# Splitting the last transfer of values in a streaming attention decode kernel

## The chip, the cores and the metric

The kernel runs on one core of one Trainium2 chip. The metric is the device time of one execution in microseconds (us), given as the median of several executions. A profile is one further execution, taken by the hardware profiler; its span (first to last instruction) is 1.7 to 1.9 us shorter than the device time. All times of landings and of single instructions below are from the records of such a trace, counted from the start of its span. A transfer has landed when the shares of all sixteen DMA engines have arrived: in the trace of the kernel before each of the last five values transfers has sixteen landings, 3.59 to 3.71 us from first to last. The record names different chips for different calls of runs (4, 2, 14 and 10), so times are compared with the kernel before in the same rounds; the traces, one per kernel, are from several chips.

## The reference, cut to what matters

Two attention decode steps with one query position and batch 4, their outputs concatenated. Part A has 32 query heads over 8 shared key/value heads and looks at the last 2048 positions; part B has 32 heads of its own and looks at all 8192. B is nearly all of the work: its two caches are 537 MB in bf16, every byte is used once, and the work on it is a matrix-vector product per head.

```python
q = (x @ wq).reshape(B, 1, 32, 128).transpose(0, 2, 1, 3)
scores = einsum("bhqd,bhkd->bhqk", q, k_cache) * 128 ** -0.5
o = einsum("bhqk,bhkd->bhqd", softmax(scores), v_cache)
out = o.transpose(0, 2, 1, 3).reshape(B, 1, 32 * 128) @ wo
```

## The kernel before

Part B goes in 64 chunks of two heads of one batch entry. A chunk is 128 tiles of keys and 128 tiles of values; a tile is 128 partitions x 128 values in bf16, so a chunk of keys or of values is 4 MB, one row of 32 KB for each partition. The sync queue (SP) issues all large loads. PE transposes the key tiles, multiplies them with the query, and multiplies the value tiles of the chunk before with its probabilities.

The last chunk of values has no later work to hide behind. It comes in five transfers with a semaphore each, so that PE can follow the stream:

```python
LASTV = (64, 32, 16, 8, 8)
...
def dma_kv(kind, c):
    ...
    if kind == "v" and c == NC - 1:
        j0 = 0
        for i, n in enumerate(LASTV):
            x = slice(j0 * P, (j0 + n) * P)
            sch.add_dma("sp", lambda e, x=x: e.dma_start(dst[:, x], src[:, x]), "d_vl%d" % i, waits=waits, key=("vl", j0))
            j0 += n
        return
...
def emit_pv(c, g):                       # eight products of a value tile with probabilities
    ...
    for t in range(TG):
        j = g * TG + t
        ...
        if c == NC - 1:
            waits += [("vl", j)] if ("vl", j) in sch.tk else []
        pe_mm(po[:, base:base + n], tile_of("v", c, j), pbt[...][:, c % NPB, j * UC:j * UC + n],
              start=j == 0, stop=j == ch["NT"] - 1, waits=waits, ...)
```

After its issues, the sync queue does one more thing. It waits for the output weights and for the last piece of keys (`kl`), and then raises a semaphore without which PE may not do the output product of an earlier chunk pair, in the middle of the last chunk's keys:

```python
dma_kv(kind, c)
if kind == "v" and c > NCA and (c - NCA) % 2 == 1:
    hp = max(0, c - NCA - 2) // 4
    sch.add("sp", lambda e: e.sem_inc(sems["eng_sp"], 1), waits=[("wos", hp)] + (["kl"] if c == NC - 1 else []),
            key=("wos2", c - 2 if c > NCA + 1 else NONE), self_inc=True)
```

## Time and profile before

| | before |
|---|---|
| time, median of 3 | 1374.14 us (1374.09 to 1374.22) |
| span of the profiled execution (its time was 1374.43 us) | 1372.6 us |
| HBM read, rate over the span | 587.21 MB, 428 GB/s |
| last values transfer landed, in the trace | 1369.060 us |
| last product of a value tile started | 1369.326 us |

The lines themselves are in the prediction. They are read from the outside in: the front page says which resource is busy all the time (the DMA engines), the chain of work says what the end hangs on (the last transfer), and the timeline says what is still to do when that has landed (eight products and a fixed rest). In a line of the chain or timeline the first number is the start and the second the duration, xN is a count, and brackets hold the idle time just before and what ended it. PE is the matrix unit, PEld its weight load, DVE, ACT and POOL are the vector, scalar and GpSimd engines; SPq is the sync queue, and a DMA_DIRECT2D there is the issue of a transfer. The end of a matmul is modelled, so each one shows 0.19 us although they start some 0.03 us apart. This hides short idle times.

### The profile page before, as it was taken

How to read it: one execution, taken by the hardware profiler on the slowest of the kernel's cores; microseconds unless marked ns; L12 is line 12 of the kernel's file. 1: busy time of each engine (PE TensorE's matmuls, PEld its weight loads, DVE VectorE, ACT ScalarE, POOL GpSimd, SP SyncE). 2: the span in 40 equal slices, each digit the busy share in tenths (PEclk: the TensorE clock that was granted, in tenths of full speed). 3: DMA queues.
4: the chain of work that ended last, by engine and by line, in shares of the span. 5: the costliest groups of instructions: out<-in, count | busy, mean ns of one | idle time of the engine just before them, and what ended most of it. 6: DMA issues, size and time to landing. Idle time of an engine off the chain costs nothing.

```text
span 1372.6 us, 59967 instructions
## 1 busy us (share of the span) xinstructions
PE 1176.5 (86%) x27065; PEld 1132.9 (83%) x27067; DVE 656.6 (48%) x1434; ACT 434.7 (32%) x650; POOL 7.3 (1%) x28
## 2 busy tenths in 40 slices
PE   4888898889888888988888888888898888888888
PEld 4777898888888888888888878888898888888888
DVE  1775454445444444454445444444454444444544
ACT  1553232333223322332233323322333233323322
POOL 2000000000000000000000000000000000000000
PEclk9998999999999999999999999999999999999999
DMA  9999999999999999999999999999999999999998
GB/s 400 423 424 432 429 433 428 433 432 432 432 431 433 429 434 428 434 430 434 430 434 430 430 433 432 432 431 433 429 433 431 434 429 434 430 432 432 432 427 352
DMA packets 25261, 587.53 MB, mean 428 GB/s; under 512 B 2820, under 2 KB 2840, under 8 KB 6296
## 3 DMA queue, kind: packets, MB, share of 16 engines
q1 hardware_dynamic: 25208, 587.22, 99.8%
q8 instruction: 16, 0.26, 0.1%
q14 instruction: 5, 0.04, 0.0%
q10 hardware_dynamic: 32, 0.01, 0.0%
HBM read 587.21 MB, written 0.01 MB: 428 GB/s over the span
## 4 chain that ended last, share of the span: by engine, by line
DMA 65%; PE 33%; issue 1%; DVE 1%; ACT 0%; SPq 0%; DVEq 0%
DMA kv<-in_B_k_cache_dram 57%; PE tr L408 21%; PE sc L410 9%; DMA kv<-in_A_k_cache_dram 5%; DMA kv<-in_B_v_cache_dram 3%; PE po L410 2%; PE fin L410 1%; PE ms L410 0%; ACT kt L476 0%; DVE sA L527 0%; SPq L365 0%; ACT pba L597 0%; PE ms L408 0%; DVE zA L683 0%; DVE rm L536 0%
## 5 line engine op out<-in xcount | busy, mean ns | idle before, releaser
L408 PE MATMUL tr<-identb,kv 128*128 128x128 bf16 x8704 | 697.9, 230 | 148.8 <-DMA kv<-in_B_k_cache_dram 141.5
L478 DVE COPY kt<-tr 128x1024 bf16<-128x1024 bf16 x736 | 502.6, 690 | 457.1 <-PE tr L408 452.7
L408 PEld LDWEIGHTS tr<-identb,kv 128*128 128x128 bf16 x8704 | 552.9, 104 | 165.2 <-DMA kv<-in_B_k_cache_dram 81.7
L476 ACT ACTIVATE kt<-tr 128x1024 bf16<-128x1024 bf16 x352 | 359.3, 1023 | 666.8 <-PE tr L408 666.7
L410 PE MATMUL sc<-qb,kt 128*128 128x64 bf16 x8704 | 446.2, 196 | 14.3 <-ACT kt L476 12.8
L410 PEld LDWEIGHTS sc<-qb,kt 128*128 128x128 bf16 x8704 | 366.4, 100 | 26.0 <-ACT kt L476 20.2
L410 PE MATMUL po<-pbb,kv 128*128 128x64 bf16 x8320 | 284.4, 192 | 4.5 <-issue 3.9
L410 PEld LDWEIGHTS po<-pbb,kv 128*128 128x128 bf16 x8320 | 263.2, 97 | 7.1 <-issue 4.1
L577 ACT ACTIVATE pbb<-sc,negb 64x128 bf16<-64x128 f32 x128 | 51.6, 403 | 254.3 <-DVE negb L564 253.5
L541 DVE TENSOR_REDUCE rm<-sc 64x1 f32<-64x128 f32 x128 | 37.0, 289 | 56.6 <-PE sc L410 55.7
L553 DVE TENSOR_REDUCE gm<-ms 1x2 f32<-1x128 f32 (+1 forms) x72 | 20.1, 279 | 48.4 <-PE ms L408 48.4
L564 DVE COPY negb<-ms 128x1 f32<-128x1 f32 (+1 forms) x72 | 11.4, 158 | 47.0 <-PE ms L410 46.8
L410 PE MATMUL ms<-identf,gx 1*128 1x1 f32 (+1 forms) x144 | 27.2, 256 | 0.8 <-DVE zA L683 0.8
L666 DVE TENSOR_TENSOR oz<-po,rz 128x8 bf16<-128x8 f32 x33 | 5.5, 166 | 40.7 <-PE po L410 40.7
L410 PEld LDWEIGHTS ms<-identf,gx 1*128 1x128 f32 (+1 forms) x144 | 21.1, 182 | 4.6 <-DVE zA L683 0.9
L577 ACT ACTIVATION_READ_ACCUMULATOR pbb<-sc,negb 64x1 f32 x128 | 23.7, 185 | 0.0
L410 PE MATMUL po<-pba,kv 128*128 128x64 bf16 x512 | 20.5, 199 | 3.5 <-issue 2.1
L410 PEld LDWEIGHTS po<-pba,kv 128*128 128x128 bf16 x512 | 17.9, 102 | 5.7 <-ACT pba L597 4.2
L408 PE MATMUL ms<-identf,rm 128*1 128x128 f32 (+1 forms) x72 | 19.5, 271 | 2.4 <-DVE rm L536 2.3
L557 DVE TENSOR_SCALAR gx<-gm 1x128 f32<-1x128 f32 (+1 forms) x72 | 16.0, 222 | 2.5
L683 DVE CAST zB<-ms 64x8 bf16<-64x8 f32 x64 | 10.5, 164 | 9.2 <-PE ms L410 8.7
L410 PE MATMUL ms<-xT,kv 128*128 128x4 bf16 x256 | 7.1, 166 | 8.8 <-DMA kv<-in_A_wq_dram 5.0
(61 smaller groups left out, 173.9 us busy)
## 6 DMA issues: line engine op xcount, KB each, us to landing
kv<-in_B_k_cache_dram SPq DMA_DIRECT2D x63, 4096.0 KB, 26.5
kv<-in_B_v_cache_dram SPq DMA_DIRECT2D x63, 4096.0 KB, 30.9
kv<-in_A_k_cache_dram SPq DMA_DIRECT2D x8, 2048.0 KB, 14.8
kv<-in_A_v_cache_dram SPq DMA_DIRECT2D x8, 2048.0 KB, 16.2
kv<-in_A_wq_dram SPq DMA_DIRECT2D x1, 4096.0 KB, 12.5
kv<-in_B_wq_dram SPq DMA_DIRECT2D x1, 4096.0 KB, 27.1
wor<-in_A_wo_dram SPq DMA_DIRECT2D x8, 512.0 KB, 9.8
wos<-in_B_wo_dram SPq DMA_DIRECT2D x16, 256.0 KB, 20.3
```

Of the source, the lines that this page charges most:

```text
L408: sch.add("pe", lambda e: e.transpose(o, l, r), waits, key)
L410: sch.add("pe", lambda e: e.matmul(o, l, r, start=start, stop=stop), waits, key)
L476: sch.add("act", lambda e: e.activation(dst, src, ACTF.Copy), waits=waits, key=("ev", s))
L478: sch.add("dve", lambda e: e.tensor_copy(dst, src), waits=waits, key=("ev", s))
L541: sch.add("dve", lambda e, src=src, pp=pp: e.tensor_reduce(out=rm[pp, m, 0:1], in_=src, axis=AX.X, op=ALU.max), waits=[("S", ch["s_last"]) ...
L553: sch.add("dve", lambda e: e.tensor_reduce(out=gm[0:C, m, 0:U], in_=src, axis=AX.X, op=ALU.max), waits=[("trm", c)], key=("gmax", c))
L557: sch.add("dve", lambda e: e.tensor_scalar(out=dst, in0=gv, scalar1=-scale, scalar2=None, op0=ALU.mult), waits=[("gmax", c)], key=("gx", c))
L564: sch.add("dve", lambda e: e.tensor_copy(negb[:, m, 0:C], ms[:, col:col + C]), waits=[("bc", c)], key=("negb", c))
L577: sch.add("act", lambda e, src=src, pp=pp, n=n, u=u: e.activation(probs_of(c)[pp, :, u], src, ACTF.Exp, bias=negb[pp, m, 0:1], scale=scale ...
L666: sch.add("dve", lambda e: e.tensor_tensor(out=o, in0=i0, in1=i1, op=ALU.mult), waits=waits, key=("oT", c))
L683: sch.add("dve", lambda e, src=src, pp=pp: e.tensor_copy(z[pp, :].rearrange("p (r b) -> p r b", r=k), src), waits=[("sm", c)] + free if h ...
```

## The change

The intent: the work behind the last landing is eight products. If the last eight tiles come in two transfers of four, the first four can be multiplied while the last four are on their way. The whole change is one line; the transfers, their semaphores and PE's waits all follow from it.

```diff
-LASTV = (64, 32, 16, 8, 8)
+LASTV = (64, 32, 16, 8, 4, 4)
```

## The prediction

> **What bounds the kernel now.** I read the front page first, then the list of transfers, then the chain of work that ended last, and at the end the timeline and the stretches of the last ten microseconds. The front page says what fills the span:
>
> ```profile
> span 1372.6 us, 59967 instructions
> PE 1176.5 (86%) x27065; PEld 1132.9 (83%) x27067; DVE 656.6 (48%) x1434; ACT 434.7 (32%) x650; POOL 7.3 (1%) x28
> DMA  9999999999999999999999999999999999999998
> HBM read 587.21 MB, written 0.01 MB: 428 GB/s over the span
> ```
>
> The DMA engines are busy 90% or more of every slice but the last, and move 428 GB/s from start to end; PE is below them at 86%. So the kernel is a stream of 587 MB, and the time is that stream plus a lead-in plus what is left to do after the last byte. The change touches no bytes and no stage but the last. The chain of work, asked for the last 73 us, shows that tail:
>
> ```profile
> 1329.92 39.14 DMA kv<-in_B_v_cache_dram
> 1369.06 0.05 issue
> 1369.11 0.42 PE po L410 x8
> ...
> 1369.62 0.18 DVE oz L666
> 1369.80 0.04 issue
> 1369.84 0.40 PE fin L410 x4
> 1370.24 0.02 issue
> 1370.27 0.42 DVE outB L724
> ```
>
> The reader is to see that the end hangs on the landing of the fifth and last values transfer (1329.92 + 39.14 = 1369.06), and that what follows is a fixed chain of 3.5 us: eight value products, the normalisation, four output products, one copy, the store. Only the first of these, 0.42 us, is what the change can shorten. The timeline of the same stretch, PE alone:
>
> ```profile
> 1366.85 2.03 PE L410 MATMUL po<-pbb,kv 128*128 128x64 bf16 x56
> 1369.11 0.41 PE L410 MATMUL po<-pbb,kv 128*128 128x64 bf16 x8 [0.23 <-DMA kv<-in_B_v_cache_dram]
> ```
>
> PE has caught up with the stream: it is idle 0.23 us before the last eight. The merged row of 56 hides two smaller stops. In the single records inside it, the products of tiles 104, 112 and 120 carry the waits for the last three transfers. Those transfers land in full at 1367.780, 1368.422 and 1369.060, and the products start at 1367.828, 1368.470 and 1369.107, 0.047 to 0.048 us later each time. So over the last 24 tiles PE runs at the pace of the landings.
>
> The stretches of 1 us show that the end of the stream is thin:
>
> ```profile
> 1364.00:1365.00 1.00, 1.00 (x33) 1.00 (x33) 0.35 (x2) 0.00 (x0) 0.00 (x0) 1.00 1.00 399
> 1366.00:1367.00 1.00, 0.95 (x14) 0.53 (x11) 0.00 (x0) 0.38 (x1) 0.00 (x0) 1.00 0.57 229
> 1367.00:1368.00 1.00, 1.00 (x39) 1.00 (x36) 0.69 (x1) 0.22 (x1) 0.00 (x0) 1.00 0.46 176
> 1368.00:1369.00 1.00, 0.88 (x24) 0.64 (x20) 0.00 (x0) 0.00 (x0) 0.00 (x0) 1.00 0.13 45
> ```
>
> The last two columns are the busy share of the 16 DMA engines and GB/s. They fall from 1.00 to 0.13 because the engines finish unevenly: the sixteen landings of the last transfer run from 1365.468 to 1369.060, a spread of 3.59 us. The last engine alone decides. What counts is therefore its packet time, and not the bandwidth of the core.
>
> [...] sixteen landings per transfer, and the product starts 0.047 us after the last of them. [...] on the last engine the 8 packets and the completion packet of the transfers with 8, 4 and 2 KB rows take 2.478, 1.249 and 0.642/0.638 us; less 9 ns for the completion packet and divided by 8, these are 308.6, 155.0 and 78.9 ns a packet, a line of 76.1 ns per 2 KB plus 2.8 ns. [...] No transfer here has 1 KB rows, so that stays an extrapolation. [...] the transfers are issued 39 us before they land.
>
> **The change, part by part.** It replaces one transfer of eight tiles (128 rows of 2 KB, 256 KB) by two of four (128 rows of 1 KB, 128 KB), each with its own semaphore, and PE waits at tiles 120 and 124 instead of at 120.
>
> Removed from the path behind the last byte: four products. The single records have the first of the eight at 1369.107, the fourth at 1369.210 and the eighth at 1369.326. With only four left, the last starts 0.103 us after the landing is seen, not 0.219: a gain of 0.116 us. The wait rides on the weight load of tile 124, as it does for tiles 112 and 120 now, so I expect no new PE instruction.
>
> Added to the stream: on the last engine 16 packets of 1 KB and two completion packets in place of 8 of 2 KB and one. By the line above, a 1 KB packet takes 38.05 + 2.8 = 40.9 ns, a transfer 8 x 40.9 + 9 = 336 ns, both 672 ns, against 640 now. The last landing moves by +0.03 us.
>
> Does PE get to the last four in time? The first four would land at 1368.422 + 0.336 = 1368.758. The last product of tiles 112 to 119 started at 1368.688, so PE starts tile 120 at 1368.805 and the fourth of these at 1368.908. The last four land at 1369.094 and start at 1369.141; the last of them starts at 1369.244 against 1369.326 now. Net **-0.08 us**.
>
> Moved: one more issue on the sync queue. The first four of the five cost 0.43 us each; the fifth does not:
>
> ```profile
> 1329.92 6.12 SPq L365 DMA_DIRECT2D kv<-in_B_v_cache_dram  x1
> ```
>
> I read this as a queue of transfers that is full until an older one has drained; it frees at 1336.04, just after the small weight transfer ahead (256 KB) has landed on its first engine, at 1335.949. The sixth issue will block too. If it needs nine more packets drained on the fastest engine, that is 1343.3 (the first landing of the next key transfer); on the slowest, between 1339.6 and 1347.0. None of this matters for the bytes, which are wanted at 1368. It would matter only for the step that the sync queue takes next:
>
> ```profile
> SPq L395 <- DMA kv<-in_B_k_cache_dram: 13.4, 1, 13.4
> ```
>
> It waits for the last piece of keys, which lands at 1349.44, and then lets PE go on to the output product at 1354.24. An issue that is done by 1349.4 costs nothing, one done by 1354 costs nothing either.
>
> **The rivals.** (a) *The shorter rows cost more than the line says.* Each 10 ns more per 1 KB packet is 16 x 10 = 0.16 us on the last engine and would eat the gain twice over. For it: 1 KB is outside what the trace holds. Against it: the line through 8, 4 and 2 KB is straight, with 2.8 ns of fixed cost[...]. If a 1 KB packet took as long as a 2 KB one, the last landing would be 0.64 us later and the kernel about 0.53 us slower: 1374.7. (b) *The sync queue stays blocked past 1354*, for instance until the values transfer ahead has begun to land at 1355.45 or has landed at 1359.16. Then the output product and the last transposes behind it start 1.2 to 5 us late. Of this PE gets back its idle time before the last products (0.5, 0.23 and the short stops), so 1 to 4 us would remain: 1375 to 1378. Against it: the fifth issue was let go when 1 to 2 transfers had drained, not when six had. I give this 4 in 100. (c) *It is all hidden.* If PE were still behind at tile 120, landing earlier would be worth nothing; but PE waits at 104, 112 and 120 now, so it isn't behind. (d) *The two completion signals land further apart*[...]; then the first four products start late, and still have 0.3 us of slack before the last four land. No effect on the end.
>
> **Range and chances.** The sum is 1374.14 - 0.116 + 0.033 = 1374.06 us. Its parts are uncertain by about 0.1 us: the gain is bounded by 0.12 us if the new packets cost nothing more, and lost if each of the 16 costs 5 ns more than the line. The three times before lie within 0.13 us, but the profiled execution of the same kernel took 1374.43, so another session can differ by 0.3 us, and the stream itself (587 MB) repeats only as well as that. I take 1373.4 to 1374.8. A change of 2% would be 27 us. The whole chain behind the last byte is 3.5 us, and even rival (b) at its worst is 4 us, 0.3%. Nothing I can name reaches 2%, so "within 2%" gets 0.985[...].
>
> **What would show each step right or wrong.** In the profile after: (1) the same 587.21 MB and 428 GB/s, one more values transfer in the list of issues, two of 128 KB and one of 256 KB; (2) packets under 2 KB up by 256 plus 16 completions, those under 8 KB up by 128 + 16; (3) in the timeline the last row of products x4 after the wait on the values transfer, with some 0.3 us from its start to its end in place of 0.41; (4) the last landing 0.02 to 0.06 us later relative to the landing of tile 112, that is 0.66 to 0.70 us behind it in place of 0.638; (5) PE idle before tile 120 as well as before tile 124, the two starts 0.34 us apart; (6) two long issues on the sync queue, the second done before 1350. Wrong would be: a gap of 0.8 us or more between the landing of tile 112 and the last one (rival a), or the output product near 1354 moved to a later time with PE idle before it (rival b). The prediction would also be wrong if the sum of the kernel before this tail were to move, by a different start of the stream or a different pace of its loop; I see no line of the change that does that.

(Passages that no trace of this case shows are cut out of the recorded texts, here and below, at the marks. No term of the forecast's sum is among them: 1374.14 - 0.116 + 0.033 = 1374.06 us stands, with both terms worked out from records of the kernel before. Against rival (a) the straight line through three row sizes is all that is left; the small transfers of inputs and outputs do hold twelve packets of 1 KB, median 46 ns, which it overlooks. That the issue of 6.12 us was held by a full queue is inference from that one issue; the runs below do not bear it out in this form.)

## The result, and the profile after

The changed kernel took 1374.12 us, median of 5 runs (1374.01 to 1374.33), the kernel before 1374.22 us in 5 runs (1374.09 to 1374.29). The ratio of the fast runs is 1.0, with a 95% interval of 0.9985 to 1.0014. So the two are the same by time. The difference of the medians, -0.10 us, is close to the -0.08 that was expected, but it is smaller than the spread of either kernel, and by itself it proves nothing.

The front page after, lines that answer to those of before (which are in the prediction):

```profile
span 1372.4 us, 59968 instructions
PE 1175.4 (86%) x27065; PEld 1132.5 (83%) x27067; DVE 656.3 (48%) x1434; ACT 435.2 (32%) x650; POOL 7.4 (1%) x28
DMA packets 25405, 587.53 MB, mean 428 GB/s; under 512 B 2836, under 2 KB 3112, under 8 KB 6440
HBM read 587.21 MB, written 0.01 MB: 428 GB/s over the span
```

The stream is the same, and PE has not one instruction more. The packets under 512 B went from 2820 to 2836, those under 2 KB from 2840 to 3112: 16 completion packets (4 B, 9 ns each in the records) and 256 rows of 1 KB, as the prediction listed.

The chain of work after, from 1366 us on:

```profile
1366.08 0.81 PE tr L410 x3
1366.89 1.48 PE po L410 x48
1368.36 0.01 issue
1368.38 0.96 PE po L410 x16
...
1369.43 0.18 DVE oz L666
1369.61 0.04 issue
1369.65 0.40 PE fin L410 x4
1370.06 0.02 issue
1370.08 0.42 DVE outB L724
```

This view misleads. It names PE alone where before it named the landing, as if PE were now the bound. The single records say otherwise: products wait at tiles 112, 120 and 124 and start at 1368.379, 1368.763 and 1369.031, each 0.046 us after a landing (1368.333, 1368.717, 1368.985). From the last product before a stop to the first after it are 0.165 to 0.205 us, about the 0.19 us that a matmul is shown with, so the rows run together and the chain sees at most 0.01 us of idle time. The timeline of PE does the same:

```profile
1366.73 2.60 PE L410 MATMUL po<-pbb,kv 128*128 128x64 bf16 x64
1369.65 0.38 PE L410 MATMUL fin<-wol,oz 128*4 128x256 bf16 x4 [0.33 <-DVE oz L666]
```

Before there was a row of 56 and, after 0.23 us of idle time, a row of 8. Now there is one row of 64.

The sync queue, its fifth and sixth issue (the fifth is the one that took 6.12 us before), in two lines that belong to two windows:

```profile
1331.09 5.38 SPq L365 DMA_DIRECT2D kv<-in_B_v_cache_dram  x2
```

```profile
1335.97 0.49 SPq L365 DMA_DIRECT2D kv<-in_B_v_cache_dram  x1
```

The first line is both of them, the second the sixth alone. The fifth is blocked as before (4.83 us), the sixth is not.

Where did the time go? I split the end of each trace at points that do not depend on how early the stream came: the landing of the first 64 tiles of the last values, the last landing, and the start of the last product.

| from the records | before | after | difference | predicted |
|---|---|---|---|---|
| landing of the first 64 tiles | 1364.053 | 1363.934 | -0.119 | 0 |
| from there to the last landing | 5.007 | 5.051 | +0.044 | +0.033 |
| from the last landing to the start of the last product | 0.266 | 0.149 | -0.117 | -0.116 |
| from there to the end of the span | 3.234 | 3.242 | +0.008 | 0 |

The gain is there, of the size foreseen: -0.117. The +0.044 fits the cost foreseen, but is about as large as the 0.04 us to which that row repeats (below). And the first row, which the change cannot touch, differs by just as much as the gain. Over all the traces but the padded one (1364.55) the landing of the first 64 tiles lies anywhere between 1363.7 and 1364.1 us in kernels with the same stream. That is the noise in which the gain drowns.

### The profile page after: what moved, and what is told of

Its sections match the earlier page's. It is cut to its first block, busy times and chain, and to the rows that moved or that the text cites. A ratio compares the mean times of both kernels' runs of the same rounds, so it can differ in the third digit from the quotient of the medians.

```text
span 1372.4 us, 59968 instructions
## 1 busy us (share of the span) xinstructions
PE 1175.4 (86%) x27065; PEld 1132.5 (83%) x27067; DVE 656.3 (48%) x1434; ACT 435.2 (32%) x650; POOL 7.4 (1%) x28
## 2 busy tenths in 40 slices
DMA packets 25405, 587.53 MB, mean 428 GB/s; under 512 B 2836, under 2 KB 3112, under 8 KB 6440
## 4 chain that ended last, share of the span: by engine, by line
DMA 60%; PE 37%; DVE 1%; issue 1%; ACT 1%; SPq 0%; DVEq 0%
DMA kv<-in_B_k_cache_dram 54%; PE tr L408 22%; PE sc L410 9%; PE po L410 3%; DMA kv<-in_B_v_cache_dram 2%; DMA kv<-in_B_wq_dram 2%; PE fin L410 1%; DMA kv<-in_A_k_cache_dram 1%; PE ms L410 1%; DVE sA L527 1%; ACT kt L476 0%; ACT pba L597 0%; DVE rm L536 0%; PE ms L408 0%; DVE sA L525 0%
## 6 DMA issues: line engine op xcount, KB each, us to landing
kv<-in_A_wq_dram SPq DMA_DIRECT2D x1, 4096.0 KB, 12.4
```

## The experiments

The theory: the gain is the products taken from behind the last landing, about 0.03 us each; the cost is about 0.03 us for the shorter rows; nothing else moves. The main rivals: the shorter rows or the smaller last transfer change the landing itself; products behind the landing are hidden; more issues on the sync queue hold up something else.

A table of all traces first; the runs are told below. "Landing" is the time from the landing of the first 64 tiles to the last landing; "products" the time from the last landing to the start of the last product. The pad run, which has the end of the kernel before, shows how well these repeat: 4.972 against 5.007, and 0.264 against 0.266. By this one pair the second column is good to 0.002 us and the first only to some 0.04. With rows of 256 B the first is worse: the run with eight of 1 and the signal unmoved, left out of the table because PE came late to its products, has 5.887 where the same transfers have 5.691 below.

| last transfers, in tiles | landing | products | time, median | before, same rounds |
|---|---|---|---|---|
| ... 16, 8, 8 (before) | 5.007 | 0.266 | | |
| ... 16, 8, 4, 4 (the change) | 5.051 | 0.149 | 1374.12 | 1374.22 |
| ... 8, 4, 4, one wait | 5.042 | 0.268 | 1374.25 | 1374.12 |
| ... 16, 16 | 4.971 | 0.502 | 1374.27 | 1374.12 |
| 64, 64 | 4.871 | 1.906 | 1375.68 | 1374.12 |
| ... 16, 12, 4 | 5.015 | 0.181 | 1373.98 | 1374.12 |
| ... 8, 4, 2, 2 | 5.091 | 0.084 | 1374.08 | 1374.05 |
| ... 8, 2, 2, 2, 2 | 5.123 | 0.085 | 1374.08 | 1374.22 |
| ... 8 and eight of 1, signal moved | 5.691 | 0.046 | 1374.62 | 1374.22 |
| ... 8, 8, GpSimd padded | 4.972 | 0.264 | 1374.73 | 1374.15 |

### The split without the earlier products

```diff
-"d_vl%d" % i, waits=waits, key=("vl", j0))
+"d_vl%d" % min(i, 4), waits=waits, key=("vl", j0) if i < 4 else ("vl", NTB - 8) if i == 5 else None)
```

(Only the end of the changed line is shown.) The two transfers of four share a semaphore, and the products from tile 120 on wait for both.

> The last eight tiles come in two transfers of four as in the change, but both count on one semaphore and the products of all eight wait for both: the split without the earlier products. Theory (the gain is four products taken from behind the last landing, the split itself costs a little): the last landing stays 0.65 us behind the landing of tile 112, as in the changed kernel, eight products follow it, the last starts 0.219 us after the first; time 0.00 to 0.04 us above the kernel before, so about 0.1 us above the changed kernel. Rival (shorter rows or a smaller last transfer help the landing itself): the last landing comes earlier and the time is that of the changed kernel, 0.1 us below the kernel before.

Measured: 1374.25 us (5 runs, 1374.18 to 1374.32) against 1374.12 for the kernel before (9 runs). In the trace the last landing is 0.663 us behind that of tile 112, and the last product starts 0.268 us after it; from the landing of the first 64 tiles to the last product it is 0.037 us more than before, inside the 0.00 to 0.04 expected (the 0.13 of the medians is not, but lies in the noise). The timeline of PE shows the old picture again, eight products after a wait:

```profile
1369.09 0.41 PE L411 MATMUL po<-pbb,kv 128*128 128x64 bf16 x8 [0.26 <-DMA kv<-in_B_v_cache_dram]
```

So the split alone gains nothing, and no help to the landing is seen. Between this run and the change lie 0.119 us in the second column: that is the four products and only they.

### The change in the other direction, small and large

```diff
-LASTV = (64, 32, 16, 8, 8)
+LASTV = (64, 32, 16, 16)
```

> The last two transfers of eight tiles merged into one of sixteen (4 KB rows): the change in the other direction. Theory: sixteen products follow the last landing, the last starts 0.455 us after the first in place of 0.219; the last landing 1.249 us behind that of tile 96 in place of 1.280; sum +0.205 us against the kernel before, about 1374.42. Rival (products behind the landing are hidden or make up for it elsewhere): within 0.05 us of the kernel before.

```diff
-LASTV = (64, 32, 16, 8, 8)
+LASTV = (64, 64)
```

> The last 64 tiles in one transfer: the same, magnified. Theory: 64 products follow the last landing, 63 gaps of 0.0288 us = 1.82 us in place of 0.219; the landing 0.11 us earlier because of fewer packets; sum +1.5 us against the kernel before, about 1375.7. Rival (the end is set by something else than products behind the landing): under 0.5 us.

Measured: with sixteen 1374.27 us, 0.15 above the kernel before in the same rounds; by the trace 5.473 us from the first landing to the start of the last product in place of 5.273, +0.200 where +0.205 was expected. With sixty-four 1375.68 us (one of its five runs took 1377.28, the others 1375.54 to 1375.78), 1.56 above the kernel before; by the trace 6.777 us, +1.504 where +1.5 was expected. The timeline of PE with sixty-four:

```profile
1368.85 2.05 PE L410 MATMUL po<-pbb,kv 128*128 128x64 bf16 x64 [1.96 <-DMA kv<-in_B_v_cache_dram]
1371.22 0.38 PE L410 MATMUL fin<-wol,oz 128*4 128x256 bf16 x4 [0.33 <-DVE oz L666]
```

PE is idle for 1.96 us and then has all 64 products before it, one every 29.5 ns (1.86 us for 63 gaps). This is the run in which the effect stands clear of the noise: each of its five times lies over a microsecond above all nine of the kernel before (ratio 1.0014, interval 1.0 to 1.0028). Products behind the last landing cost their full time, and the same line goes through 4, 8, 16 and 64 of them.

### Twelve and four: the small last transfer without one more transfer

```diff
-LASTV = (64, 32, 16, 8, 8)
+LASTV = (64, 32, 16, 12, 4)
```

> Twelve and four tiles in place of eight and eight: a last transfer of four tiles as in the change, but no transfer more than the kernel before. Theory: last landing as in the kernel before within 0.02 us, four products behind it; the twelve products (0.33 us) just fill the time between the two landings, so the last four start at most 0.03 us late; sum -0.09 us against the kernel before, the same as the changed kernel within 0.03. Rival (the change gains through the extra stop of PE between two small transfers): as the kernel before.

Measured: 1373.98 us (5 runs, 1373.95 to 1374.23) against 1374.12; in the trace -0.077 us from the first landing to the last product. The last four start 0.093 us after the landing in place of 0.046, because PE is still busy with the twelve. That is a little more than the 0.03 us that was allowed for; as they then follow the twelve without a stop (0.088 us from the first of their starts to the last, where it is 0.103 in the change), the last of them is only 0.032 us later than in the change. It is as good as the change (-0.077 against -0.073 us by the trace), with one transfer less. The two extra stops of PE have no merit of their own; what counts is how few products are left.

### Beyond the change: 4, 2, 2 and eight of one

```diff
-LASTV = (64, 32, 16, 8, 8)
+LASTV = (64, 32, 16, 8, 4, 2, 2)
```

> Four, two and two tiles: one step beyond the change. Theory: 336 + 2 x 184 = 704 ns from the landing of tile 112 to the last one, 0.066 more than before; two products follow, the last starts 0.04 after the first in place of 0.219; sum -0.11 us against the kernel before, -0.03 against the changed kernel: by the trace (landing of the first 64 tiles to the start of the last product) 5.16 us against 5.273 and 5.200. By time not to be told from the changed kernel. Rival (landings of very small transfers cost more each): 5.25 or more.

Measured: 1374.08 us against 1374.05; by the trace 5.175 us, where 5.16 was expected. The rows of 512 B land 0.177 to 0.179 us apart (0.184 expected), so the line of packet times still holds there. Of what the two products less give (0.065), the landing takes back most (0.040). By time the step can't be seen.

```diff
-LASTV = (64, 32, 16, 8, 8)
+LASTV = (64, 32, 16, 8, 1, 1, 1, 1, 1, 1, 1, 1)
```

> The last eight tiles in eight transfers of one tile (rows of 256 B): the change driven to its end, with seven transfers more than the kernel before. Theory (line of packet times, 2.8 ns plus 76.1 ns per 2 KB): a transfer takes 8 x 12.3 + 9 = 107 ns, all eight 0.86 us in place of 0.638, one product follows in place of eight; from the landing of the first 64 tiles to the start of the last product 5.22 to 5.37 us against 5.273 before: gain and cost cancel, time within 0.1 us of the kernel before. Rival 1 (rows below 512 B cost as much as rows of 512 B, 21.8 ns a packet): 1.47 us for the eight, the kernel 0.6 us slower, 1374.8. Rival 2 (the sync queue is blocked by the many issues until past 1354): the output product near 1354 starts late, 1 us or more slower. Without it all twelve issues are done by 1349.

Measured: 1385.81 us (5 runs, 1385.30 to 1386.10) against 1374.05. That is 11.8 us slower, a hundred times the gain that was at stake (0.1 us). Rival 2 was right: the issues were not done by 1349. Rival 1 came true as well (the eight transfers landed over 1.514 us, where it said 1.47; of rows of values below 512 B only those of 256 B were run), but is hidden behind the wait. The list of PE's waits in the last 45 us, and the chain of work from 1331 to 1365 us:

```profile
PE fin L410 <- SPq L395: 10.6, 1, 10.6
PE tr L408 <- DMA kv<-in_B_k_cache_dram: 1.6, 1, 1.6
```

```profile
1330.98 4.72 SPq L365
...
1335.75 0.49 SPq L365
...
1336.29 0.43 SPq L365
...
1336.76 16.61 SPq L365
...
1353.41 5.43 SPq L365
...
1358.88 3.01 SPq L365
...
1361.94 1.65 SPq L365
...
1363.63 0.89 SPq L365
...
1364.57 0.03 SPq L395
1364.60 0.04 issue
1364.64 0.59 PE fin L410 x4
```

Each SPq L365 line is one issue. The first small one is blocked for 4.72 us, two go through in 0.49 and 0.43 us, and the fourth is blocked for 16.61 us, until 1353.37. From there on every issue waits. The sync queue comes to its signal (L395) only at 1364.6, and PE, which was ready for the output product (fin) near 1354, has stood still for 10.6 us. From there to the last product it takes 1.0 us longer than in the kernel before: its granted clock is 0.50 from 1364.6 to 1369 us, where it was 1.00 before the wait, and eight transposes take 0.85 us in place of 0.45. All data of the last values had landed by 1369.6, but PE was only then at the transposes of the last keys.

### Is it the signal? And is it a count?

Two runs tell apart what in the eight transfers did the harm. In the first the sync queue does its wait and its signal after the third small issue, the rest of the issues stay as they are (cut: the line of `LASTV`, which is that of the eight transfers):

```diff
                     j0 += n
+                    if i == 6:
+                        sch.add("sp", lambda e: e.sem_inc(sems["eng_sp"], 1), waits=[("wos", max(0, c - NCA - 2) // 4), "kl"],
+                                key=("wos2", c - 2), self_inc=True)
 ...
-            if kind == "v" and c > NCA and (c - NCA) % 2 == 1:
+            if kind == "v" and NCA < c < NC - 1 and (c - NCA) % 2 == 1:
```

> The eight transfers of one tile again, but the sync queue does its wait for the last keys and its signal to PE after the third of the small issues, before the one that was blocked for 16.6 us. Theory (the 11.7 us of the eight transfers came from that signal being stuck behind blocked issues, and nothing else): PE has no long wait at the output product near 1354, the time is 1374.7 to 1374.9, that is 0.66 us above the kernel before, all of it from rows of 256 B that land 0.186 us apart as seen in the run before. Rival (the blocked issues themselves hold up the transfers, or PE): 1377 or more. The issues stay blocked as before.

Measured: 1374.62 us (1374.47 to 1374.66, 4 runs) against 1374.22. The 10.6 us are gone, and the list of PE's waits no longer has the sync queue in it:

```profile
PE tr L411 <- DMA kv<-in_B_k_cache_dram: 1.6, 1, 1.6
PE po L413 <- DMA kv<-in_B_v_cache_dram: 0.5, 1, 0.5
PE sc L413 <- ACT kt L479: 0.4, 2, 0.2
PE fin L413 <- DVE oz L669: 0.3, 1, 0.3
```

The later issues are still blocked (until 1353.5, 1359.0, 1362.0 and so on), and that harms nothing, since their data is wanted much later. So the loss came from what stood behind the issues in the same queue. The remaining +0.40 us (+0.464 by the trace: 0.684 later landing, 0.220 fewer products) is that of the 256 B rows: the eight transfers land 0.15 to 0.17 us apart (0.186 in the run before, which I had taken for the estimate; hence 0.1 us under my range), where the line of packet times would have 0.107. A row of 256 B is hardly cheaper than one of 512 B (0.177 to 0.179 us for a transfer above).

In the second, four transfers of two tiles:

```diff
-LASTV = (64, 32, 16, 8, 8)
+LASTV = (64, 32, 16, 8, 2, 2, 2, 2)
```

> The last eight tiles in four transfers of two (rows of 512 B), one transfer more than 4, 2, 2, where no issue after the first was blocked. Theory 1 (a count of transfers in flight blocks: the fourth one behind the first long block waits, as with rows of 256 B): the fourth small issue is blocked from 1336.8 to about 1353.4, the signal to PE comes at 1353.4 to 1353.5, still ahead of the output product at 1354.1, so no loss: 0.1 us under the kernel before. Theory 2 (the block is a matter of the 256 B rows): no second long issue. Tail from the landing of the first 64 tiles to the start of the last product: 0.178 x 4 in place of 0.638, two products in place of eight: 5.17 us against 5.273.

Measured: 1374.08 us (1373.98 to 1374.18, 4 runs) against 1374.22. The fourth small issue, in the timeline of the sync queue:

```profile
1336.75 16.60 SPq L365 DMA_DIRECT2D kv<-in_B_v_cache_dram  x1
```

It is blocked for 16.60 us, until 1353.36, with rows of 512 B just as with 256 B. So it isn't the row size, nor the bytes of a transfer. In the run with 4, 2, 2 the second and third small issue went through at once (0.49 and 0.43 us), so two issues more than the kernel before are free, and the third more is held. PE's signal then comes at 1353.435 and the output product starts at 1353.883. There was 0.45 us to spare. One more transfer was not run, but in the run with eight of one the issue after this one was held for another 5.43 us, far more than that. What is counted stays open: each of these transfers has 128 rows, so a limit on transfers and one on rows look the same here. The probe below speaks against a plain count of transfers: of its small ones, with 1 to 15 rows, twelve had been issued by 1352.71 us, at 0.25 to 4.2 us for each issue, where with 128 rows the fourth was held until 1353.4. From the first landing to the last product it takes 5.208 us, where 5.17 was expected and 5.175 was had with one transfer less.

### Why the last engine comes last

The last landing is set by one of sixteen DMA engines, the one that comes 3.2 to 3.8 us after the first when the first 64 tiles land (4.06 in the padded run below). A probe asked which engines lie behind. In the changed kernel, the last four tiles came in sixteen transfers of 1, 2, 3 ... 15 and 8 partitions (cut: the new semaphores and PE's waits for them).

```diff
+PROBE = [(n * (n + 1) // 2, n + 1) for n in range(15)] + [(120, 8)]
 ...
+                    if i == len(LASTV) - 1:
+                        for k, (p0, m) in enumerate(PROBE):
+                            sch.add_dma("sp", lambda e, x=x, p0=p0, m=m: e.dma_start(dst[p0:p0 + m, x], src[p0:p0 + m, x]), "d_p%d" % k, key=("vp", k))
+                        break
```

> A probe, not a candidate: the last four tiles come in sixteen transfers of 1, 2, 3 ... 15 and 8 partitions, each with its own semaphore[...]. Theory (the lag of the last engines was set long before, by instruction fetches on single engines): each engine has one constant lag between 0 and 3.7 us, and the sets of landings grow by one engine from transfer to transfer. Rival (the lag follows from the order of rows in the transfer itself): the landings of a small transfer lie together and early. The time is not of interest, some 1 us above the kernel before.

Measured: 1378.38 us in its one run. The sets of landings do grow by one engine from transfer to transfer. Some of them, in us from the start of the span (the first entry of each set, which came at the issue, is left out; the output's transfers of 4 rows at the end of the kernel before show the like, five landings each, the first 0.44 to 0.55 us after the issue began):

```
1 partition:   1365.73
2 partitions:  1365.91 1366.10
3 partitions:  1365.41 1366.09 1366.27
4 partitions:  1365.59 1366.27 1366.44 1367.59
5 partitions:  1365.76 1366.44 1366.61 1366.86 1367.77
6 partitions:  1365.95 1366.62 1366.79 1367.05 1367.95 1368.56
7 partitions:  1366.12 1366.81 1366.96 1367.24 1368.14 1368.77 1369.02
```

Each engine comes again about 0.18 us later in each row, so each has a lag of its own; which of the sixteen they are these times do not show. The sixth and seventh lie 2.7 and 2.9 us behind the third, the first two 0.7 and 0.8. Transfers of 128 rows do not even them out: over the last five of the kernel before the spread stays at 3.59 to 3.71 us. One that gives the late engines fewer rows was not tried. The rival (a lag that follows from the order of rows) is refuted: the late landings of these small transfers lie 1 to 3 us apart. The extra time of this run has a plain cause that was at hand: its sixteen issues too held the sync queue's signal back, to 1357.7, and PE waited 3.5 us for it.

Where does the lag come from? In the trace of the kernel before the spread of the sixteen landings is 0.79 us for the first transfer, at 13 us. It steps up to 1.97 at 29 us, 2.33 at 39, 3.29 at 134 and 3.85 at 144 us, and then stays between 3.6 and 3.9 to the end. In that time, between 20 and 167 us, one instruction queue (q8) fetches 15 packets of 16 KB, each of which takes 0.98 to 1.11 us, and after that none until 1368. To test this, 768 short memsets of an unused tile were put on GpSimd:

```diff
+        pad = sb("pad", [P, 768], BF16)
 ...
+        for i in range(768):
+            sch.add("pool", lambda e, i=i: e.memset(pad[:, i:i + 1], 0.0))
```

> The kernel before with 768 short memsets of an unused tile on GpSimd in the first 100 us, some 48 KB more instructions, off every path. Theory (the 3.6 us by which the last DMA engine ends behind the first were set by instruction fetches that each held up one engine early on): three more packets of 16 KB on the instruction queue, each early; the lags of the sixteen landings of the last values transfers change by 1.0 to 1.8 us on one to three engines while the others keep theirs; if one of those is among the seven that lie 3.0 us or more behind, the whole kernel takes 1.0 to 1.8 us (or more, if the same engine takes two) longer, else the time stays. Rival (the lag is a property of the engines or of the rows): pattern and time as before, within 0.2 us.

Measured: 1374.73 us (1374.62 to 1374.94, 4 runs) against 1374.15 (7 runs, 1374.06 to 1374.86). The form of the fetches was not as expected. They came as six packets of 8 KB (48 KB in all) on the other instruction queue, as the page's section on queues shows, where it was 5 packets in the kernel before:

```profile
q8 instruction: 16, 0.26, 0.1%
q14 instruction: 11, 0.09, 0.0%
```

The six started between 12.4 and 38.9 us. In just that time the lag of the last engine went 0.99, 1.45, 3.08, 3.56, 4.21 us over the first five transfers, where it was 0.79, 0.77, 1.97, 1.83, 2.33 before, and four engines instead of three lay over 1.5 us behind by then. In the last full transfer the spread is 4.04 us in place of 3.71 (3.23 to 3.77 in the other traces). The median rose by about 0.6 us, with one of the seven runs of the kernel before (1374.86) inside the padded kernel's range. That is less than the 1.0 us that I had put as the least; the guess, which was not shown, is that the engine that was hit is not the one that ends last in the kernel before, so that part of its lag is hidden behind that one's. This is one pad and one trace.

A count in the trace of the kernel before says more. Eight of the fifteen 16 KB fetches start between 19.7 and 71.2 us. After the first two, 2 engines land more than 1.2 us after the first one; after those at 34.8, 43.6, 51.4, 57.7, 64.8 and 71.2 us it is 3, 4, 5, 6, 7 and 8. Then no such fetch comes until 127.3 us, and the count stays at 8. Seven more follow, and after the last, at 167.1 us, seven engines lie 3.1 to 3.85 us behind. So with each of the six fetches from 34.8 to 71.2 us one more engine fell behind, and stayed behind. That a fetch sets back the one engine that carries it is inference: which fetch falls on which engine was not shown. The spread of 0.79 us is there at 13 us, before the first of them at 19.7; its source stays open.

## Why the prediction was right, point by point

**The bound.** The kernel is a stream, and the change touches only what follows the last landing. The rate over the span stayed at 427 to 428 GB/s in every run but the one with eight transfers and a late signal (424). The end of the stream moved by up to 0.3 us from trace to trace (0.5 with the pad), more than the change is worth, so only the intervals behind it show the change.

**The gain of 0.116 us** was measured as 0.117 between the two traces and as 0.119 against the split with one wait. The line from 4 to 64 products confirms what it rests on.

**The cost of 0.03 us.** The trace has +0.044, the split with one wait +0.035. Both fit 0.03, but neither stands clear of the 0.04 to which this column repeats, so the cost is not resolved by them. The last landing came 0.652 us after that of tile 112, a little under the 0.66 to 0.70 that was named, and above the 0.638 of before. The packet of 1 KB takes 46 ns in the records; two transfers in 652 ns make it 39.6 ns by the landings ((652 - 18) / 16), where 40.9 was worked out.

**PE in time for the last four.** Right in the end, wrong in a detail: the two starts lie 0.268 us apart, not 0.34, because the first four landed 0.384 us after tile 112 and the last four 0.268 us after them. The sum is what the line gives; why it was shared so unevenly in that one trace is open (in the run with 4, 2, 2 the first four took 0.351). Rival (d) had allowed for landings further apart, and for no effect on the end.

**The issue on the sync queue.** Here a step of the prediction failed. It said that the sixth issue "will block too". It did not: 0.495 us. Sign (6), two long issues, failed with it. The reading behind it, a queue that frees one place per drained transfer, is too simple. After the one long block (4.6 to 6.1 us over the traces) two issues of 128 rows pass at once (0.43 to 0.50 us each), and only the next is held, for 16.6 us, until 1353.4 to 1353.5, with rows of 512 B as with rows of 256 B. The conclusion (no cost) held, but not by this reasoning: the change has one issue more, and two were free. A sixth issue that did block would have cost nothing either, if it was let go at 1353.4 as the held one with four twos was. Rival (b) was given 4 in 100 for this change and 1 to 4 us; it is real, came with seven more transfers, and cost 11.8 us, because I had looked for a release at 1355 or 1359 and the signal came at 1364.6.

**Rival (a)**, costlier short rows, is not seen at 1 KB (two transfers in 0.652 us, 0.672 by the line) and at 512 B (0.176 to 0.193 us a transfer, 0.184 by the line). It is true at 256 B: 0.15 to 0.21 us a transfer, which less 9 ns and divided by 8 is 18 to 25 ns a packet, where the line has 12.3.

**What the profile would show.** The counts of packets were exact. The row of four products with an idle time before it never appeared, since the profile merges stops of about the modelled length of a matmul (0.165 to 0.205 us from start to start, against 0.19). A forecast in terms of merged rows was the wrong form; single records were needed.

**The range.** 1373.4 to 1374.8 was wide against the spread in rounds (1374.0 to 1374.3). The medians of the kernel before alone went from 1374.05 to 1374.22. That the medians differ by 0.10 where 0.08 was forecast is luck: the noise is larger than either.

What stays open: the rule by which the sync queue's issues are held and let go, and what it counts; which fetch falls on which engine; and why the landing of the first 64 tiles moves by some 0.3 us between runs.

## What to carry to other kernels

What was left to do behind the last byte of this stream cost its full time (29.5 ns a product with 64 of them), so make the last transfer small; but the gain levels off when more, smaller transfers cost what the fewer products save (here at two to four tiles: 5.200, 5.175 and 5.208 us with 4, 4, with 4, 2, 2 and with four twos), and it is worth only the few products removed, 0.1 us of 1374. Before splitting, look in the trace for long issues: here issues that were held, one of them for 16.6 us, held everything behind them in their queue, and PE stood still for 10.6 us, so put no signal that an engine needs soon behind a burst of issues. And measure a change of this size by intervals within the trace that start after the noise, and by a magnified version of it (64 tiles in place of 4), not by the total time.
